# Alternate loading at the start of an attention and MLP block, and where transposed maxima are placed

## The chip, the cores and the metric

The kernel runs on one core of a Trainium2 chip. Its engines work side by side, each through its own instructions in order: TensorE (PE in the profile: matmuls and transposes), VectorE (DVE), ScalarE (ACT), GpSimd (POOL) and SyncE (SP, which here issues all DMAs). The metric is the time of one execution in microseconds on the device; smaller is better. Before the change the median of three runs is 1664.54 us (1664.17 to 1665.02).

## The reference

One transformer block on x of 2048 rows and 512 columns, in float32: layer norm, attention with 32 heads of 16 columns, a residual, layer norm, an MLP with 1792 hidden columns and SiLU, a residual.

```python
def _A_ref(x, wqkv, wo):
    qkv = (x @ wqkv).reshape(B, S, 3, H, Dh)...   # q, k, v per head
    scores = jnp.einsum("bhqd,bhkd->bhqk", q, k) * Dh ** -0.5
    p = _softmax(scores, axis=-1)
    o = jnp.einsum("bhqk,bhkd->bhqd", p, v)
    return o (heads side by side) @ wo

def _B_ref(x, w1, w2):
    return _silu(x @ w1) @ w2

h = x + _A_ref(_layernorm(x), wqkv, wo)
h2 = h + _B_ref(_layernorm(h), w1, w2)
```

## The kernel before, in words

**Precision.** Projections, the output projection and the MLP are made in three products each: an operand is split into a high part (a cast to fp32r, suffix `_h`) and a low part (the operand less its high part, suffix `_l`, made by `low`), and `product` (L123) adds high x high, low x high and high x low over four chunks of 128. Scores are made in float16 from q and k split in the same way and stored three times along the contraction.

**The softmax's maxima.** Before an item (four heads by 512 queries) can be scored, the maximum of each row of its scores is found: `maximum` (L241) makes a 128x512 block of scores into a bank of PSUM (`ps_m`) and DVE reduces it into a column of `mx`. Where all blocks of an item are there, `finish_max` joins the columns and splits the result into two float16 parts (`ns`) on POOL. `place_max` (L287) then transposes `ns` on TensorE into a bank (`ps_n`), copies it to SBUF (`mt`), and SP writes it as two more rows of q (`qs`), so that the matmul of the scores subtracts the maximum itself. In all there are 64 items of 32 to 64 blocks and 33 placements.

**Phases.** First comes block 0 of x (four tiles of 128 rows): statistics, normalization, transposes, and its products with the values' weights. Then `project_qk` and `project_v` run over blocks and column groups. Then come 512 groups of attention, interrupted three times by the output projection and `mlp` for a finished block of rows (`marks`), and a last MLP. The order of work is written out by hand: every instruction of an engine stays in the order of the program (`keep_in_program_order`). Maxima are strewn in between as bursts: `weave` (L381) calls `burst` (L375) after the k-th matmul of a product. `BESIDE_A` puts six maxima behind the sixth of twelve matmuls of a projection; `BESIDE_C` puts three behind the fifth and the twelfth of the first MLP product of a hidden chunk and four behind the eighth of its second product. The banks of kind `sm`, which maxima and `ps_n` take in turn, are six in the later projections and three from attention on.

**When a placement is due.** `one_max` (L340) hands `place_max` to `soon` (L313) outside attention groups, three steps ahead; `tick` (L317), called at the beginning of each projection, each hidden chunk of an MLP and each group, then calls it, ahead of the first matmul of that step. Within attention groups the table `late` does it.

**The start.** `load_x(0, parts=4)` issues four transfers of 256 KB, then come four of the values' weights (`raw_v`), eight of the weights of k and q, and block 1 of x. `idle` makes transposes of the identity that nobody reads. `first_rows(t)` normalizes tile t on DVE and calls `turn_high` (four transposes on TensorE, a copy to `xth` on ACT); `first_products` adds high x high for a tile of rows and some chunks. The high part of the weights, `wv_h`, is made on ACT for chunks 0 and 1 and on POOL for 2 and 3.

Of the kernel before, what the change touches and what calls it, by code (L numbers as in the profile page):

```python
# [20 lines left out]
P = 128  # L21
# [60 lines left out]
def attention_mlp_kernel(ctx: ExitStack, tc: tile.TileContext, x, wqkv, wo, w1, w2, out):  # L82
# [204 lines left out]
    def place_max(piece):  # L287

        i, a = piece
        ns = split.pop(piece)  # L290
        n = ns.shape[1]
        ps = bank("ps_n", "sm", F16)
        tr(ps[:n, :P], ns, ident_h)
        mt = small.tile([32, P], F16, name="mt")[:n]
        if at["attention"]:
            dve("tensor_copy", mt, ps[:n, :P])
        else:
            act("copy", mt, ps[:n, :P])
        for j in range(2):
            dst = qs[i % RING][64 * j + 48:64 * j + 50, slice(None) if a is None else slice(a, a + 1)]  # L300
            dst = dst.rearrange("r a n -> r (a n)").rearrange("r (a b) -> r a b", b=P)
            pin(nc.sync.dma_start(dst, mt[n // 2 * j:n // 2 * (j + 1), :]))
        placed.add(piece)
# [4 lines left out]
            for i in range(ITEMS) for j in range(2)}  # L308
    END = 64 * ITEMS
    at = {"item": 0, "done": 0, "half": 0, "step": 0, "due": 0, "attention": False, "group": None, "ready": 0, "next": 0, "blocks": True}  # L310
    agenda, late = {}, {}

    def soon(steps, fn, *a):  # L313

# [2 lines left out]
    def tick():  # L317
        at["step"] += 1
        for step in [step for step in late if step < at["step"]]:

            finish_rest()
            for i in late.pop(step):
                place_max(i)
        for fn, a in agenda.pop(at["step"], ()):
            fn(*a)

# [13 lines left out]
    def one_max(half=None, ps=None):  # L340

        i = next_item()
        if i == ITEMS:
            return
        if half is None:
            half = at["half"]
            at["half"] = 1 - half
        if at["blocks"]:

            i = min(range(2), key=lambda n: (todo[n, half] or todo[n, 1 - half] or [(n, KC)])[0][1])  # L350
        elif not todo[i, half] and 64 * (i + 2) <= at["ready"] and KC * i - at["next"] > 12:

            i += 1
        half = half if todo[i, half] else 1 - half
        at["done"] += 1
        block = todo[i, half].pop(0)
        piece = piece_of(i, block[3])
        found_all = maximum(*block, ps)

        finish_rest()  # L360
        if found_all:
            steps = due_at(piece)
            g = at["group"]
            if g is None or g + 1 in marks:
                soon(steps, place_max, piece)
                finish_max(piece, g is not None)
                return
            late.setdefault(at["step"] + steps, []).append(piece)
            if steps == WAIT:
                unfinished.append(piece)  # L370
                found_at["step"] = at["step"]
            else:
                finish_max(piece, False)

    def burst(n, *more):  # L375
        for ps in more:
            one_max(ps=ps)
        for _ in range(n - len(more)):
# [29 lines left out]
    with ExitStack() as pa:  # L408
# [88 lines left out]
            turn(xts[b][:, t, :], xth[b][:, :, t * P:(t + 1) * P], xtl[b][:, :, t * P:(t + 1) * P],  # L497
                 "sm" if b == 1 else "st")

        load_x(0, parts=4)  # L500
        for dc in range(DC):
            dma(raw_v[:, dc, :], wqkv[dc * P:(dc + 1) * P, 2 * D:])
        for key in (1, 0):
            for dc in range(DC):
                dma(raw_qk[key][:, dc, :], wqkv[dc * P:(dc + 1) * P, key * D:(key + 1) * D])
# [15 lines left out]
            act("copy", xth[b][:, :, columns(t)], ps)  # L521
            return ps

        idle(24)
        found = [statistics(xts[0][:, t, :]) for t in range(2)]
        turned, ps_vs = [], []

        def first_rows(t):
            normalize(xts[0][:, t, :], xts[0][:, t, :], *found[t])
            turned.append(turn_high(0, t))  # L530

        def first_products(t, *chunks):
            if t == len(ps_vs):
                ps_vs.append(bank("ps_v", "st" if t < 3 else "sm"))
            for c in chunks:
                mm(ps_vs[t], xth[0][:, c, columns(t)], wv_h[:, c, :], start=c == 0, stop=False)

        first_rows(0)
        idle(8)
        for c in range(2):  # L540
            act("copy", wv_h[:, c, :], raw_v[:, c, :])
        found += [statistics(xts[0][:, t, :]) for t in range(2, 4)]
        for c in range(2, 4):
            pool("tensor_copy", wv_h[:, c, :], raw_v[:, c, :])
        first_rows(1)
        first_products(0, 0)
        first_rows(2)
        first_products(0, 1)
        first_rows(3)
        for chunks in ((0, 1), (2,), (3,)):  # L550
            for t in range(2):
                if t or chunks != (0, 1):
                    first_products(t, *chunks)
        for t in range(2, 4):
            first_products(t, *range(DC))
        for c in range(DC):
            low(wv_l[:, c, :], raw_v[:, c, :], wv_h[:, c, :])
        for t in range(4):
            low(xtl[0][:, :, columns(t)], turned[t], xth[0][:, :, columns(t)])

        keys = [n for n in range(NG) if n % 2]
# [8 lines left out]
                normalize(xts[1][:, t - 1, :], xts[1][:, t - 1, :], *found.pop(t - 1))  # L570
        for t in range(4):
            for c in range(DC):
                mm(ps_vs[t], xth[0][:, c, columns(t)], wv_l[:, c, :], start=False, stop=False)
                mm(ps_vs[t], xtl[0][:, c, columns(t)], wv_h[:, c, :], start=False, stop=c == DC - 1)
            act("copy", va[:, t, :, 0:DH], ps_vs[t].rearrange("p (h d) -> p h d", d=DH))
            if t == 0:
                load_x(2)
# [625 lines left out]
```

## Time and profile before

| | |
|---|---|
| median of three runs | 1664.54 us |
| profiled execution | 1664.61 us, span 1662.8 us |
| TensorE busy, matmuls | 1649.5 us, 99% of the span |
| DVE busy | 1453.2 us, 87% |
| ACT busy | 1235.6 us, 74% |
| POOL busy | 396.7 us, 24% |
| placements: copies `mt` on DVE / ACT | 30 / 3 |

A row of the timeline gives start, duration, engine, line, operation, what it writes and reads, and a count; in brackets stands how long the engine had been idle before it and what ended that. Nearly all matmuls go through one helper line, so they are told apart by the names of their tiles. Matmuls overlap: the duration of one (0.39 us for a 128x512 one in fp32r) is longer than its distance to the next (0.23 us), and the distances between starts are what counts. In the chain (the work that ended last, followed back), a piece such as "PE pv L89 x7" is seven matmuls in sequence.

### The profile page before, as it was taken

What the parts mean: (1) busy time and instruction counts of PE and PEld (TensorE: products, weight loads), DVE (VectorE), ACT (ScalarE), POOL (GpSimd) and SP (SyncE); (2) the same over time, 40 slices, a digit from 0 to 9 for tenths busy, and PEclk for the clock granted to TensorE, in tenths of its full rate; (3) what the DMA queues carried; (4) which work ended last, traced back from release to release, by engine and by line L of the source; (5) the groups of instructions that cost most, each with busy time, mean ns of one, the idle gap of its engine ahead of it and who ended that gap; (6) DMA issues with size and microseconds to landing.
All of it is one profiled execution on the core that took longest, in us unless ns stands there. A gap on an engine that the chain in (4) does not pass through costs nothing.

```text
span 1662.8 us, 28572 instructions
## 1 busy us (share of the span) xinstructions
PE 1649.5 (99%) x10551; PEld 649.5 (39%) x10551; DVE 1453.2 (87%) x2403; ACT 1235.6 (74%) x2435; POOL 396.7 (24%) x584
## 2 busy tenths in 40 slices
PE   9999999999999999999999999999999999999999
PEld 7666422222245532222245532222245642222387
DVE  7899999999988889999988889999978769999443
ACT  5323799999953389999952379999962389999743
POOL 5423311211234301211244311211235311111100
PEclk9999999999999999999999999999999999999999
DMA  5444411211232211121222111121232211100222
GB/s 199 109 100 140 120 32 37 57 33 36 69 76 67 58 50 34 41 51 33 60 76 79 58 50 32 37 58 32 61 68 77 69 50 34 33 12 21 65 77 82
DMA packets 104408, 102.85 MB, mean 62 GB/s; under 512 B 22736, under 2 KB 81168, under 8 KB 104268
## 3 DMA queue, kind: packets, MB, share of 16 engines
q1 hardware_dynamic: 104268, 101.02, 22.4%
q8 instruction: 83, 1.36, 0.4%
q14 instruction: 57, 0.47, 0.1%
HBM read 77.72 MB, written 17.29 MB: 57 GB/s over the span
## 4 chain that ended last, share of the span: by engine, by line
PE 91%; DVE 4%; ACT 3%; issue 1%; DMA 1%; POOL 1%; SPq 0%; DVEq 0%; POOLq 0%
PE pv L89 35%; PE ps_s L89 21%; PE ps_m L89 11%; PE ps_acc L89 10%; PE ps_qk L89 5%; PE ps_wo L89 3%; PE ps_w L89 3%; ACT pt L103 3%; PE ps_v L89 3%; DVE mx L253 2%; PE ps_tr L92 1%; SPq L109 0%; DVE pvs L106 0%; POOL ri L96 0%; PE ps_n L92 0%
## 5 line engine op out<-in xcount | busy, mean ns | idle before, releaser
L253 DVE TENSOR_REDUCE mx<-ps_m 128x1 f32<-128x512 f32 x2011 | 1261.2, 684 | 79.5 <-PE ps_m L89 50.2
L103 ACT ACTIVATE pt<-ps_s 128x512 f32<-128x512 f32 x2048 | 1010.9, 609 | 32.0 <-PE ps_m L89 18.6
L89 PE MATMUL pv<-pt,va 128*17 128x512 f32 x4096 | 537.6, 598 | 1.4 <-DVE pv L106 0.5
L89 PE MATMUL ps_s<-qs,ks 64*128 64x512 f16 x2048 | 532.1, 379 | 2.8 <-ACT pt L103 1.6
L89 PE MATMUL ps_m<-ks,qs 48*128 48x512 f16 x2011 | 504.8, 380 | 0.9 <-DVE mx L253 0.7
L89 PEld LDWEIGHTS <-ks 64*128 64x128 f16 x2048 | 150.2, 95 | 547.2 <-issue 434.2
L96 POOL TENSOR_TENSOR ri<-rc,minus 128x16 f32<-128x16 f32 x31 | 90.8, 2929 | 306.1 <-DMA rc<-dn 306.1
L89 PEld LDWEIGHTS pv<-pt,va 128*17 128x17 f32 x4096 | 69.0, 95 | 215.3 <-issue 201.6
L89 PEld LDWEIGHTS <-qs 48*128 48x128 f16 x2048 | 119.0, 94 | 63.4 <-issue 57.3
L103 ACT CAST w2h<-w 128x512 fp32r<-128x512 f32 x56 | 34.7, 619 | 99.5 <-PE ps_acc L89 99.5
L103 ACT ACTIVATE g<-pv 128x512 f32<-128x512 f32 x39 | 23.3, 597 | 100.5 <-PE pv L89 100.5
L89 PE MATMUL ps_acc<-w2l,gh 128*128 128x512 f32 x224 | 92.8, 414 | 0.0
L89 PE MATMUL ps_acc<-w2h,gh 128*128 128x512 f32 x224 | 91.9, 410 | 0.0
L96 POOL TENSOR_TENSOR w2l<-w,w2h 128x512 fp32r<-128x512 f32 x42 | 53.9, 1283 | 148.2 <-ACT w2h L103 148.2
L89 PE MATMUL ps_acc<-w2h,gl 128*128 128x512 f32 x224 | 88.2, 394 | 0.0
L106 DVE TENSOR_TENSOR gl<-g,gh 128x512 fp32r<-128x512 f32 x53 | 37.2, 701 | 56.2 <-ACT gh L103 56.2
L103 ACT ACTIVATE ks<-ps_qk,qk_s 128x512 f32<-128x512 f32 x30 | 20.7, 689 | 68.8 <-PE ps_qk L89 66.9
L96 POOL TENSOR_SCALAR nm<-nm 128x16 f32<-128x16 f32 (+1 forms) x50 | 12.7, 254 | 232.2 <-DVE nm L264 229.2
L89 PE MATMUL pv<-htl,w1h 128*128 128x512 f32 x156 | 65.5, 420 | 0.0
L89 PE MATMUL pv<-hth,w1h 128*128 128x512 f32 x156 | 62.4, 400 | 0.0
L89 PE MATMUL pv<-hth,w1l 128*128 128x512 f32 x156 | 61.4, 393 | 0.0
L96 POOL TENSOR_TENSOR w1l<-w,w1h 128x512 fp32r<-128x512 f32 x42 | 54.2, 1291 | 11.1 <-ACT w1h L103 11.1
(138 smaller groups left out, 1395.3 us busy)
## 6 DMA issues: line engine op xcount, KB each, us to landing
w<-in_B_w_dram SPq DMA_DIRECT2D x112, 256.0 KB
ks<-kd SPq DMA_DIRECT2D x120, 192.0 KB
qs<-qd SPq DMA_DIRECT2D x128, 48.0 KB
kd<-sh SPq DMA_DIRECT2D x16, 256.0 KB
qd<-sh SPq DMA_DIRECT2D x16, 256.0 KB
hx<-in_A_x_dram SPq DMA_DIRECT2D x16, 256.0 KB
ot<-pvs SPq DMA_DIRECT2D x124, 32.0 KB
den<-dr SPq DMA_DIRECT2D x124, 32.0 KB
```

What stands on the lines that cost most here:

```text
L89: tc.keep_in_program_order(nc.tensor.matmul(*a, **k))
L92: tc.keep_in_program_order(nc.tensor.transpose(*a))
L96: tc.keep_in_program_order(getattr(nc.gpsimd, op)(*a, **k))
L103: pin(getattr(nc.scalar, fn)(*a, **k))
L106: pin(getattr(nc.vector, fn)(*a, **k))
L253: pin(nc.vector.tensor_reduce(mx[piece][:, j, a % n, qt, kb:kb + 1], ps, axis=AX.X, op=ALU.max))
```

## The change

Two things are changed.

At the start, x tiles and the values' weights are loaded alternately, tile 0, weights 0, tile 1, weights 1 and so on; statistics, the casts of the weights (now all four on ACT), normalization, transposes and first products are written in another order, in which the products with a tile follow its transposes closely. The low parts of the weights are made on DVE and POOL by turns, and the low products of a tile take the low part of x first and the low part of the weights after it.

Outside attention groups, a placement that is due is kept in a list (`in_bursts`). `burst` looks there first, so that `place_max` comes right ahead of the burst's maxima, between the matmuls of a product; where no burst comes in the step in which it is due, the next `tick` places it. With the condition in `place_max`, the copy to `mt` is on ACT whenever no attention group is running, in the MLPs too. Of the 33 placements, three are in projections (two of them move from the front of a projection to its burst, one to the front of the projection after), six in MLPs (two in the first hidden chunk, four in others; all move to a burst), and two more slip from the first attention group behind an MLP to the next. Six copies `mt` go from DVE to ACT.

```diff
@@ -292,7 +292,7 @@
         ps = bank("ps_n", "sm", F16)
         tr(ps[:n, :P], ns, ident_h)
         mt = small.tile([32, P], F16, name="mt")[:n]
-        if at["attention"]:
+        if at["group"] is not None:
             dve("tensor_copy", mt, ps[:n, :P])
         else:
             act("copy", mt, ps[:n, :P])
@@ -308,7 +308,7 @@
             for i in range(ITEMS) for j in range(2)}
     END = 64 * ITEMS
     at = {"item": 0, "done": 0, "half": 0, "step": 0, "due": 0, "attention": False, "group": None, "ready": 0, "next": 0, "blocks": True}
-    agenda, late = {}, {}
+    agenda, late, in_bursts = {}, {}, []
 
     def soon(steps, fn, *a):
 
@@ -321,6 +321,7 @@
             finish_rest()
             for i in late.pop(step):
                 place_max(i)
+        place_due(1)
         for fn, a in agenda.pop(at["step"], ()):
             fn(*a)
 
@@ -362,7 +363,7 @@
             steps = due_at(piece)
             g = at["group"]
             if g is None or g + 1 in marks:
-                soon(steps, place_max, piece)
+                in_bursts.append((at["step"] + steps, piece))
                 finish_max(piece, g is not None)
                 return
             late.setdefault(at["step"] + steps, []).append(piece)
@@ -372,7 +373,13 @@
             else:
                 finish_max(piece, False)
 
+    def place_due(slack=0):
+        while in_bursts and in_bursts[0][0] + slack <= at["step"]:
+            place_max(in_bursts.pop(0)[1])
+
     def burst(n, *more):
+
+        place_due()
         for ps in more:
             one_max(ps=ps)
         for _ in range(n - len(more)):
@@ -497,9 +504,9 @@
             turn(xts[b][:, t, :], xth[b][:, :, t * P:(t + 1) * P], xtl[b][:, :, t * P:(t + 1) * P],
                  "sm" if b == 1 else "st")
 
-        load_x(0, parts=4)
-        for dc in range(DC):
-            dma(raw_v[:, dc, :], wqkv[dc * P:(dc + 1) * P, 2 * D:])
+        for t in range(4):
+            dma(xts[0][:, t, :], x[t * P:(t + 1) * P, :])
+            dma(raw_v[:, t, :], wqkv[t * P:(t + 1) * P, 2 * D:])
         for key in (1, 0):
             for dc in range(DC):
                 dma(raw_qk[key][:, dc, :], wqkv[dc * P:(dc + 1) * P, key * D:(key + 1) * D])
@@ -521,13 +528,17 @@
             act("copy", xth[b][:, :, columns(t)], ps)
             return ps
 
-        idle(24)
-        found = [statistics(xts[0][:, t, :]) for t in range(2)]
-        turned, ps_vs = [], []
+        found, turned, ps_vs = [], [], []
+
+        def first_statistics(t):
+            found.append(statistics(xts[0][:, t, :]))
 
         def first_rows(t):
             normalize(xts[0][:, t, :], xts[0][:, t, :], *found[t])
             turned.append(turn_high(0, t))
+
+        def first_weights_of(c):
+            act("copy", wv_h[:, c, :], raw_v[:, c, :])
 
         def first_products(t, *chunks):
             if t == len(ps_vs):
@@ -535,27 +546,34 @@
             for c in chunks:
                 mm(ps_vs[t], xth[0][:, c, columns(t)], wv_h[:, c, :], start=c == 0, stop=False)
 
+
+        idle(24)
+        first_statistics(0)
+        first_weights_of(0)
+        first_statistics(1)
+        first_weights_of(1)
         first_rows(0)
         idle(8)
-        for c in range(2):
-            act("copy", wv_h[:, c, :], raw_v[:, c, :])
-        found += [statistics(xts[0][:, t, :]) for t in range(2, 4)]
-        for c in range(2, 4):
-            pool("tensor_copy", wv_h[:, c, :], raw_v[:, c, :])
+        first_statistics(2)
+        first_weights_of(2)
+        first_products(0, 0, 1)
         first_rows(1)
-        first_products(0, 0)
+        first_weights_of(3)
+        first_products(0, 2)
+        first_products(1, 0, 1, 2)
+        first_statistics(3)
         first_rows(2)
-        first_products(0, 1)
+        first_products(0, 3)
+        first_products(1, 3)
+        first_products(2, *range(DC))
         first_rows(3)
-        for chunks in ((0, 1), (2,), (3,)):
-            for t in range(2):
-                if t or chunks != (0, 1):
-                    first_products(t, *chunks)
+        first_products(3, *range(DC))
+
+        for c in range(DC):
+            low(wv_l[:, c, :], raw_v[:, c, :], wv_h[:, c, :], "pool" if c % 2 else "dve")
+            if c % 2 == 0:
+                low(xtl[0][:, :, columns(c // 2)], turned[c // 2], xth[0][:, :, columns(c // 2)])
         for t in range(2, 4):
-            first_products(t, *range(DC))
-        for c in range(DC):
-            low(wv_l[:, c, :], raw_v[:, c, :], wv_h[:, c, :])
-        for t in range(4):
             low(xtl[0][:, :, columns(t)], turned[t], xth[0][:, :, columns(t)])
 
         keys = [n for n in range(NG) if n % 2]
@@ -570,8 +588,9 @@
                 normalize(xts[1][:, t - 1, :], xts[1][:, t - 1, :], *found.pop(t - 1))
         for t in range(4):
             for c in range(DC):
-                mm(ps_vs[t], xth[0][:, c, columns(t)], wv_l[:, c, :], start=False, stop=False)
-                mm(ps_vs[t], xtl[0][:, c, columns(t)], wv_h[:, c, :], start=False, stop=c == DC - 1)
+                mm(ps_vs[t], xtl[0][:, c, columns(t)], wv_h[:, c, :], start=False, stop=False)
+            for c in range(DC):
+                mm(ps_vs[t], xth[0][:, c, columns(t)], wv_l[:, c, :], start=False, stop=c == DC - 1)
             act("copy", va[:, t, :, 0:DH], ps_vs[t].rearrange("p (h d) -> p h d", d=DH))
             if t == 0:
                 load_x(2)
```

## The prediction

> **What bounds the kernel now.** I read the totals and the chain first, then the stretches that the change touches: the opening microseconds, one projection and two MLP iterations around a transposed set of maxima.
>
> ```profile
> PE 1649.5 (99%) x10551; PEld 649.5 (39%) x10551; DVE 1453.2 (87%) x2403; ACT 1235.6 (74%) x2435; POOL 396.7 (24%) x584
> ...
> PEclk9999999999999999999999999999999999999999
> ...
> PE 91%; DVE 4%; ACT 3%; issue 1%; DMA 1%; POOL 1%; SPq 0%; DVEq 0%; POOLq 0%
> ```
>
> TensorE sets the end: 91% of the chain, and its clock is full in every slice. So a change pays only where it takes a matmul, a switch of operand type, or a stall out of TensorE's order. The opening, as the timeline shows it:
>
> ```profile
> 3.57 0.69 DVE L106 BATCH_NORM_STATS2 st<-ks 128x6 f32<-128x512 f32 x1 [1.54 <-DMA ks<-in_A_x_dram]
> ...
> 6.09 0.66 PE L92 MATMUL ps_tr<-ident,ks 128*128 128x128 f32 x4
> ...
> 6.78 0.59 ACT L103 CAST xth<-ps_tr 128x512 fp32r<-128x512 f32 x1 [4.78 <-PE ps_tr L92]
> ...
> 8.13 0.66 PE L92 MATMUL ps_tr<-ident,ks 128*128 128x128 f32 x4 [0.52 <-DVE ks L106]
> ...
> 8.55 0.48 PE L89 MATMUL ps_v<-wv_h,xth 128*128 128x512 f32 x1
> ...
> 10.12 3.45 PE L89 MATMUL ps_v<-wv_h,xth 128*128 128x512 f32 x14
> ...
> 12.07 0.62 ACT L103 CAST wqk_h<-va 128x512 fp32r<-128x512 f32 x1 [1.07 <-DMA va<-in_A_wqkv_dram]
> 12.40 2.47 DVE L106 TENSOR_TENSOR xtl<-ps_tr,xth 128x512 fp32r<-128x512 f32 x4
> ...
> 13.41 0.39 PE L89 MATMUL ps_v<-wv_l,xth 128*128 128x512 f32 x1
> ...
> 20.75 1.04 PE L92 MATMUL ps_tr<-ident,ks 128*128 128x128 f32 x8
> ```
>
> The reader is to see that TensorE's real work starts at 8.13 and then never stops. From there to 20.75 it does 12 transposes and 48 products. The last 32 products take 20.75 - 13.41 = 7.34, or 0.23 each; a set of four transposes takes about 0.46 of its order (8.55 less 8.13 is 0.42, more with the switch back). 48 x 0.23 + 3 x 0.46 = 12.4 of the 12.6 us. There is nothing to save behind 8.13, only the start itself. The stretch behind it, and what the loads bring per 1.5 us slice of the first 60 us:
>
> ```profile
> 13.40:21.00 7.60, 7.60 (x36) 6.21 (x35) 7.26 (x16) 7.10 (x19) 3.03 (x7) 1.00 0.75 272
> ```
>
> ```profile
> GB/s 0 186 381 352 363 384 395 402 388 392 391 382 187 4 0 5 0 129 133 0 262 30 100 105 117 105 184 155 288 288 385 226 46 76 95 96 98 96 319 103
> ```
>
> In the window row the numbers after the length are busy times of PE, PEld, DVE, ACT and POOL: TensorE 7.60 of 7.60.
>
> **The change, part 1: the start.** Nothing is added or removed but the engine of two casts (`wv_h` 2 and 3 from POOL to ACT) and of two subtractions (`wv_l` 1 and 3 from DVE to POOL). The four tiles of x and the first four rows of weights are loaded alternately, so x tiles come as transfers 1, 3, 5, 7 instead of 1 to 4. Summing the GB/s row, 256 KB have moved at about 2.9 us, and the tile was usable at 3.57, so 0.6 behind; twelve have moved at about 10.6 and the last was used at 12.07, 1.4 behind. With lags of 0.6 to 1.4, tile x1 comes at 4.9 to 5.7, weights 1 at 5.6 to 6.4, x2 at 6.4 to 7.2, weights 2 at 7.1 to 7.9, x3 at 7.8 to 8.6, weights 3 at 8.6 to 9.4. I take the early ends first, as the first tile shows them. DVE now does both sets of statistics ahead of the first normalization: 4.95 + 0.69 + 0.18 + 0.55 puts its end at 6.35, the transposes at 6.4, and `xth` 0 at 7.65 (6.09 to 7.37 is 1.28 from transpose to usable). So products 0,0 and 0,1 start at about 7.7, 0.4 ahead of the 8.13 of now. But each later set of transposes stands right in front of the products that need it, and TensorE takes its matmuls in order. Of the 1.28 us from transposes to `xth`, the four transposes fill 0.46; behind set 1 stands one product (0.23), behind set 2 two (0.46), behind set 3 none. The stalls are 0.6, 0.36 and 0.82, 1.8 together, and they are new: now the sets at 8.13, 8.86 and 9.71 run ahead of the products. Net 1.8 - 0.4 = 1.4 later at the first product with a low part. By then everything else is there: on DVE the lows need 0.62 each (2.47 for four) and start near 9.8; the last one waits for `xth` 3 at 13.7 and ends at 14.4, while its products come after 16 others. The reordered low products (all `xtl` first, then all `wv_l`) are the same 32. ACT is the second watch: it starts `wqk_h` after `xth` 3, at 13.7 instead of 12.07, and has 7.10 of 7.60 us busy behind that. It falls 1.6 behind and TensorE 1.4, so the values' eviction may be 0.2 late, which the eight transposes cover. Late landings add up to 0.8, and full cover of the stalls would give a gain of 0.4: bounds -0.4 to +2.5. I take **+1.4**. It passes on whole: all that follows is released by TensorE until DVE's bursts of maxima at 49 us, and these are released by TensorE too.
>
> **Part 2: transposed maxima in projections.** These rows stand around one of them (`ps_n`):
>
> ```profile
> 115.53 0.82 PE L89 MATMUL ps_m<-ks,qs 48*128 48x512 f16 x6
> ...
> 117.89 0.23 PE L92 MATMUL ps_n<-ident_h,ns 128*32 128x128 f16 x1
> ...
> 118.76 0.62 ACT L103 CAST sh<-ks 128x512 f16<-128x512 f32 x1
> ...
> 119.28 0.25 ACT L103 COPY mt<-ps_n 32x128 f16<-32x128 f16 x1
> ...
> 119.64 0.82 PE L89 MATMUL ps_m<-ks,qs 48*128 48x512 f16 x6
> 120.06 6.19 DVE L253 TENSOR_REDUCE mx<-ps_m 128x1 f32<-128x512 f32 x10 [0.42 <-PE ps_m L89]
> ...
> 123.34 0.83 PE L89 MATMUL ps_m<-ks,qs 48*128 48x512 f16 x6
> ```
>
> From burst to burst it is 119.64 - 115.53 = 4.11 with a `ps_n` and 123.34 - 119.64 = 3.70 without: the lone f16 transpose between fp32r products costs 0.41, and DVE then idles 0.42. Moved directly ahead of the burst, the switch is paid once, and `ps_n` adds only its own slot, 0.15 (553.12 to 553.27, below). Six banks are rotated, so only the sixth maximum needs the one of `ps_n`, 0.84 later; `mt` is done 0.26 + 0.25 after `ps_n`, as ACT's cast is over by then. Gain 0.41 - 0.15 = 0.26. Of three projections two move to a burst; the third only goes to the next boundary between projections, at no gain. **-0.5**. The queue of SP gets the two small row writes one projection later, behind two writes of q; the item that reads them starts after the projections, so I cost that at nothing.
>
> **Part 3: MLPs.** Iterations from the chain, then rows of one with a `ps_n`:
>
> ```profile
> 539.26 1.82 PE pv L89 x7
> ...
> 547.02 1.82 PE pv L89 x7
> ...
> 555.24 1.83 PE pv L89 x7
> ...
> 563.02 1.82 PE pv L89 x7
> ```
>
> ```profile
> 546.42 0.60 PE L89 MATMUL ps_m<-ks,qs 48*128 48x512 f16 x3
> ...
> 546.95 0.51 PE L89 MATMUL pv<-htl,w1h 128*128 128x512 f32 x1
> ...
> 553.12 0.22 PE L92 MATMUL ps_n<-ident_h,ns 128*32 128x128 f16 x1
> 553.27 0.51 PE L89 MATMUL pv<-hth,w1h 128*128 128x512 f32 x1
> 553.47 0.62 ACT L103 CAST w1h<-w 128x512 fp32r<-128x512 f32 x1
> ...
> 554.18 0.20 DVE L106 COPY mt<-ps_n 32x128 f16<-32x128 f16 x1
> ```
>
> Iterations take 7.76 and 7.78, the one with `ps_n` 8.22: 0.45 more. Moved to the burst after five products, `ps_n` would begin five products later, at 553.12 + 5 x 0.23 or just ahead of it, about 554.2. There are three banks here: `ps_n` and two maxima fill them, and the third maximum needs `ps_n`'s bank. Its `mt` is now on ACT: 0.26 + 0.25 + 0.05 = 0.56 after `ps_n`, where without `ps_n` the third maximum started at 0.28. So the burst is 0.28 longer, and the gain is 0.45 - 0.28 = 0.17. ACT's cast of `w1h` ends at 554.09, just ahead. Four such places: **-0.7**. Two places stand ahead of the first product of an MLP:
>
> ```profile
> 484.60 0.68 DVE L106 TENSOR_TENSOR htl<-ps_tr,hth 128x512 fp32r<-128x512 f32 x1
> ...
> 485.88 0.22 PE L92 MATMUL ps_n<-ident_h,ns 128*32 128x128 f16 x1
> ...
> 486.16 0.21 DVE L106 COPY mt<-ps_n 32x128 f16<-32x128 f16 x1 [0.89 <-PE ps_n L92]
> ...
> 487.82 0.69 DVE L253 TENSOR_REDUCE mx<-pv 128x1 f32<-128x512 f32 x1 [1.45 <-PE ps_m L89]
> ```
>
> DVE idles 0.89 and 1.45 there, so its bursts begin as much earlier as TensorE reaches them. The front loses `ps_n` and a switch (0.41), the burst of four gains 0.15; 0.25 is left each, **-0.5**. The six `mt` copies that leave DVE for ACT are worth nothing: DVE has these gaps. Two more places only slip by one attention group, between the same neighbours: nothing. The floor for all places is that eight prices vanish, 0.41 x 8 = -3.3; the ceiling is in the first rival.
>
> **Sum.** +1.4 - 0.5 - 0.7 - 0.5 = -0.3. The profiled execution took 1664.61 (span 1662.8), 0.07 above the median of 1664.54: 1664.3.
>
> **Rivals.** *Slower: the third maximum waits behind casts.* If `ps_n` reaches the six MLP bursts while ACT is in a cast, `mt` waits up to 0.62 more, and TensorE with it, as the third maximum and all products behind it are in order: 0.28 + 0.62 - 0.43 = +0.47 each, +2.8. With +1.4 and -0.5 that is +3.7, 1668.3. It needs nearly the whole cast at every place; 554.09 against 554.2 speaks against it. *Faster: places become free and the start is covered*: -3.3 - 0.4 = -3.7, 1660.9. The idle of DVE speaks for it, the three banks against. *The change of the start does nothing*, because loads, not the order, set it: 1664.6 - 1.7 = 1662.9; 8.13 waited for DVE, not for a load, which speaks against. *The clock falls in the new stalls*: with products twice as long for 16 of them, 16 x 0.23 = +3.7 on top, 1668.0; against it, TensorE already stood still 0.52 before 8.13 at full clock. The Trainium skill, "TensorE: Matmul & The Clock Gate", Part 1, has the clock halved after an idle window of about 3.4 us, and under "A second HAM failure mode" also by short idling between groups. By its second rule the start would cost some 1.7 us more, by my estimate from that window; by the first nothing. The trace agrees with the first: 0.52 idle, clock full.
>
> **How the numbers follow.** 0.2% is 3.3 us, about what a measurement of this kernel can tell from no change. My forecast with the start anywhere in its bounds, the untouched start among it, stays within that: 0.81. Free places 0.09. Casts in front 0.07, the clock 0.03. The range 1662.0 to 1666.6 takes in the start's bounds (-1.8 to +1.1 about my +1.4) with half of the places' gain missing or doubled; what it leaves out at both ends is some 0.2.
>
> **What would show it.** In the changed profile the first real product begins near 7.7, with waits on `xth` near 9, 11 and 13, and the eight transposes now at 20.75 begin near 22.1. Projection bursts with a `ps_n` stand 3.85 apart, MLP iterations with one take 8.05. The prediction is wrong if the transposes at the start find other work behind them, if x1 comes much later than 5.7, or if `mt` in the MLP starts later than 0.3 after `ps_n`.

## The result and the profile after

The changed kernel takes 1667.67 us (median of 18 runs, 1666.97 to 1668.39); the kernel before took 1664.74 us in the same sessions (18 runs, 1664.17 to 1665.22). The ratio is 1.0017, with a 95% interval of 1.0011 to 1.0024: 2.9 us slower, above the range that was predicted. The profiled executions stand 2.8 apart, 1667.41 against 1664.61, so the traces can be set beside each other.

Three lines of the page of the changed kernel, its totals, the clock and the shares of the chain:

```profile
PE 1651.3 (99%) x10551; PEld 650.8 (39%) x10551; DVE 1452.7 (87%) x2395; ACT 1238.1 (74%) x2443; POOL 398.3 (24%) x584
...
PEclk9999999999999999999999999999999999999999
...
PE 93%; DVE 3%; ACT 3%; issue 1%; POOL 0%; DVEq 0%; POOLq 0%
```

TensorE still sets the end, executes as many matmuls, and has its full clock in every slice. So the 2.8 us are stalls and switches in its order, and they can be found by following how far the changed kernel lags at the same instruction. The rows from which the table is read stand below it or in the prediction; the others are the same pieces of the chains of the two kernels.

| place (start before) | lag there, us | what it adds |
|---|---|---|
| eight transposes of block 1 (20.75) | 1.91 | +1.91 the start |
| burst ahead of the first placement in a projection (115.60), burst behind it (119.70) | 1.93, 1.72 | -0.21 |
| four projections on, burst ahead of the second (134.53) | 1.84 | +0.12 |
| burst behind the second (138.63), late projections (176.66) | 1.63, 1.67 | -0.21, +0.04 |
| first matmuls of attention (188.88) | 2.75 | +1.08 the third placement |
| first chunk of MLP 1 (483.36 to 492.62) | 2.75, 2.94 | +0.19 |
| later chunk of MLP 1 (547.02 to 555.24) | 2.95, 2.84 | -0.11 |
| first chunk of MLP 2 (861.22 to 870.49), then a later one (924.88 to 933.11) | 2.85, 3.03; 3.04, 2.93 | +0.18, -0.11 |
| attention behind MLP 2 (971.28 to 981.59) | 2.94, 2.78 | -0.16 |
| MLP 3 (1247.08), two later chunks up to 1318.37 | 2.77, 2.59 | -0.09, -0.10 |
| last output projection (1563.08 to 1575.02) | 2.59, 2.86 | +0.27 |
| last piece (1650.57) | 2.82 | |

The named steps add up to 1.91 - 0.26 + 1.08 + 0.37 - 0.41 - 0.16 + 0.27 = 2.80. The step of -0.16 comes where a placement slips by one group: in the kernel before, the first of the two rows below, it stands between float32 products of the MLP and scores; now it stands behind products with the values and takes 0.04 instead of 0.16.

```profile
974.53 0.16 PE ps_n L92
```

```profile
980.06 0.04 PE ps_n L92
```

All six traces with the changed placements there have this step, and none of the others. The +0.27 ahead of the last MLP stands in only two of these six traces, this one and that of the third placement's experiment below; the others have 0.05 or less there, so I don't count it as the work of the change, and its cause is open.

The opening, as the timeline of the changed kernel shows it:

```profile
1.53 5.38 PE L92 MATMUL ps_i<-ident 128*128 128x128 f32 x24 [1.53 <-POOL ident masks.py:199]
...
4.99 0.69 DVE L106 BATCH_NORM_STATS2 st<-ks 128x6 f32<-128x512 f32 x1 [0.56 <-DMA ks<-in_A_x_dram]
...
5.82 0.51 DVE L106 TENSOR_SCALAR ks<-ks,mv,rs 128x512 f32<-128x512 f32 x1
...
6.70 0.64 PE L92 MATMUL ps_tr<-ident,ks 128*128 128x128 f32 x4
...
8.02 0.72 PE L89 MATMUL ps_v<-wv_h,xth 128*128 128x512 f32 x2
...
8.58 0.65 PE L92 MATMUL ps_tr<-ident,ks 128*128 128x128 f32 x4
...
8.99 0.47 PE L89 MATMUL ps_v<-wv_h,xth 128*128 128x512 f32 x1
...
9.91 0.96 PE L89 MATMUL ps_v<-wv_h,xth 128*128 128x512 f32 x3 [0.45 <-ACT xth L103]
...
11.07 0.72 PE L89 MATMUL ps_v<-wv_h,xth 128*128 128x512 f32 x2
...
11.99 1.20 PE L89 MATMUL ps_v<-wv_h,xth 128*128 128x512 f32 x4 [0.20 <-ACT xth L103]
...
13.02 0.60 PE L92 MATMUL ps_tr<-ident,ks 128*128 128x128 f32 x4
...
14.29 1.19 PE L89 MATMUL ps_v<-wv_h,xth 128*128 128x512 f32 x4 [0.67 <-ACT xth L103]
15.33 1.08 PE L89 MATMUL ps_v<-wv_h,xtl 128*128 128x512 f32 x4
...
22.66 1.04 PE L92 MATMUL ps_tr<-ident,ks 128*128 128x128 f32 x8
```

Behind each set of transposes TensorE waits for `xth`. Measured by starts (a matmul's order slot is 0.23 us), the stalls are 9.91 - 8.99 - 0.23 = 0.69, 11.99 - 11.07 - 0.46 = 0.46, and 14.29 - 13.02 - 0.46 = 0.81: 1.96 together. The 32 low products behind them take 22.66 - 15.33 = 7.33 as before (7.34).

A placement in a projection, from the chain of the changed kernel:

```profile
117.53 0.75 PE ps_m L89 x6
118.28 2.99 PE ps_qk L89 x12
121.27 0.16 PE ps_n L92
121.42 0.75 PE ps_m L89 x6
122.18 2.97 PE ps_qk L89 x12
125.14 0.75 PE ps_m L89 x6
```

`ps_n` takes 0.15 of TensorE's order right ahead of the burst, and the burst is no longer for it. From burst to burst it is 121.42 - 117.53 = 3.89, where the same pieces of the kernel before give 119.70 - 115.60 = 4.10. But part of this gain is lost again: from 119.70 to 134.53, four projections without a placement took 14.83, and now they take 14.95 (121.42 to 136.37). Their products stand a few ns farther apart, and I have no cause for it. Of twice 0.21, 0.26 is left by 176.66. The last projection ahead of attention, where the third placement now stands, from the timeline of the changed kernel:

```profile
181.74 0.37 PE L89 MATMUL ps_m<-ks,qs 48*128 48x512 f16 x1 [0.23 <-DVE mx L253]
...
185.28 0.23 PE L92 MATMUL ps_n<-ident_h,ns 128*32 128x128 f16 x1
...
185.50 0.70 ACT L103 ACTIVATE ks<-ps_qk,qk_s 128x512 f32<-128x512 f32 x1
...
186.28 0.62 ACT L103 CAST sh<-ks 128x512 f16<-128x512 f32 x1
186.80 0.25 ACT L103 COPY mt<-ps_n 32x128 f16<-32x128 f16 x1
187.10 0.37 PE L89 MATMUL ps_m<-ks,qs 48*128 48x512 f16 x1 [0.41 <-ACT mt L103]
...
191.63 1.05 PE L89 MATMUL pv<-pt,va 128*17 128x512 f32 x8 [0.47 <-DVE pv L106]
```

`mt` is made 1.5 us after its `ps_n`, because ACT first does an eviction and a cast that stand ahead of it in its queue. A maximum of the same projection needs the bank of `ps_n`, and TensorE stands 0.41 for it, with the products behind it. In the kernel before, that `ps_n` stood ahead of an earlier projection and held nothing up: the lag is 1.67 on either side of that place (178.33 against 176.66, 182.04 against 180.37). The first row tells why: with `ps_n` gone from there, TensorE waits 0.23 for DVE to free a bank. The burst of three maxima there takes 1.41 to the next product (180.63 to 182.04), where it took 1.05 before (179.32 to 180.37): what left TensorE's order came back as a wait.

Last, the MLPs. For a first chunk I take the distance from the last 24 matmuls of attention's values ahead of the MLP (x24) to the second part of the first product of the chunk behind it (x7). These are the two pieces in the chain of the kernel before for MLP 1, with a placement at the front of its first chunk, and below them for MLP 3, whose first chunk has none:

```profile
483.36 2.70 PE pv L89 x24
...
492.62 1.80 PE pv L89 x7
```

```profile
1237.87 2.70 PE pv L89 x24
...
1247.08 1.82 PE pv L89 x7
```

The same two pieces of MLP 1 in the chain of the changed kernel, and below them two later iterations, the first with a placement in its burst, the second without:

```profile
486.11 2.70 PE pv L89 x24
...
495.56 1.82 PE pv L89 x7
```

```profile
549.97 1.82 PE pv L89 x7
...
558.08 1.82 PE pv L89 x7
...
565.86 1.82 PE pv L89 x7
```

Before, the first chunk took 492.62 - 483.36 = 9.26 with a placement at its front and 9.21 without any: at the front the placement cost 0.05. Now it takes 9.45. A later chunk takes 8.11 with a placement in its burst, where it took 8.22, and 7.78 without one.

### The profile page after: what moved, and what is told of

Same layout as the page of the kernel before. It is cut to its first block, busy times and chain, and to the rows that moved or that the text cites. A ratio compares the mean times of both kernels' runs of the same rounds, so it can differ in the third digit from the quotient of the medians.

```text
span 1665.6 us, 28572 instructions
## 1 busy us (share of the span) xinstructions
PE 1651.3 (99%) x10551; PEld 650.8 (39%) x10551; DVE 1452.7 (87%) x2395; ACT 1238.1 (74%) x2443; POOL 398.3 (24%) x584
## 3 DMA queue, kind: packets, MB, share of 16 engines
q8 instruction: 83, 1.36, 0.3%
## 4 chain that ended last, share of the span: by engine, by line
PE 93%; DVE 3%; ACT 3%; issue 1%; POOL 0%; DVEq 0%; POOLq 0%
PE pv L89 36%; PE ps_s L89 21%; PE ps_m L89 11%; PE ps_acc L89 10%; PE ps_qk L89 5%; PE ps_w L89 3%; PE ps_wo L89 3%; ACT pt L103 3%; PE ps_v L89 3%; DVE mx L253 2%; PE ps_tr L92 1%; DVE pvs L106 0%; PE ps_i L92 0%; PE ps_n L92 0%; DVE ot L106 0%
```

## The experiments

Medians of an experiment are set against the kernel before in the same session (1664.65, 1664.67, 1664.81 or 1664.95 us). Beside the time I use stages, which the traces show much more exactly: *start*, at which block 1's eight transposes begin (20.75 before, 22.66 after); *projections*, from there to the first matmuls of attention (168.13 before, 168.97 after); *first chunk* (9.26, 9.45) and *later chunk* (8.22, 8.11) of MLP 1, as above. The start is the exception: each trace is one execution, and the landing of the loads moves it (last section), so for the start the medians decide.

### The two parts apart

The start of the changed kernel in the kernel before, with all placements as before (the part of the diff from the loads to the low products):

```diff
-        load_x(0, parts=4)
...
+        first_statistics(0)
+        first_weights_of(0)
...
+                mm(ps_vs[t], xth[0][:, c, columns(t)], wv_l[:, c, :], start=False, stop=c == DC - 1)
```

> The kernel before with the changed start alone (loads, order, engines of the casts and low parts); placements as before. Theory: the start costs 1.9 us by the eight transposes of block 1 (20.75 to 22.66) and nothing behind it takes that back, so 1666.6 us against 1664.7, ratio 1.0011, and the third placement stands where it stood, with attention beginning 1.9 later than before (first product with the values near 190.8). Rival: the 1.1 us that the changed kernel loses between the projections and attention comes from the later start (maxima and scores falling differently), not from the placement; then this kernel is near 1667.7 and attention begins near 191.7.

Measured: 1666.59 us, +1.94 (ratio 1.0012, 1.0003 to 1.0021). Start 22.92, projections 168.14, first chunk 9.26, later chunk 8.21. So the start alone loses two thirds, all of it ahead of block 1's transposes; a later start changes nothing in the projections, which it would if the 1.08 ahead of attention were its echo.

The placements of the changed kernel with the start of the kernel before (the other part of the diff):

```diff
-        if at["attention"]:
+        if at["group"] is not None:
...
+        place_due(1)
...
-                soon(steps, place_max, piece)
+                in_bursts.append((at["step"] + steps, piece))
...
     def burst(n, *more):
+        place_due()
```

> The changed placements alone; the start as before. Theory (sum of stages read from the two traces): two projections -0.33, the third placement +1.08, two first hidden chunks +0.32, four other chunks -0.41: +0.7, so 1665.4 us, with attention beginning near 189.6 instead of 188.88. Rival: placements are worth what was forecast (-1.7, 1663.0) and the whole loss belongs to the start.

Measured: 1665.23 us, +0.58 (1.0004, 0.9995 to 1.0013); the interval holds 1, so the stages have to show it. Projections 168.94, first chunk 9.46, later chunk 8.10, the changed kernel's stages. (Block 1's transposes begin at 21.65 in this trace, though the start is that of before: statistics waited there for a late tile of x.) The steps of the table give -0.26 + 1.08 + 0.37 - 0.41 - 0.16 = +0.62. The two medians add up to +2.5 of the 2.9; the other tenths have no place.

### The third placement

In the changed kernel, this placement alone goes back to the front of the projection before:

```diff
-        place_due(1)
+        place_due(0 if in_bursts and in_bursts[0][1] == (2, None) else 1)
```

> The changed kernel, with the third placement put back in front of the last projection but one (all else as changed). Theory: its new place, ahead of the last projection's scores and maxima, costs 1.08 and its old one nothing, because DVE was the limit there: 1666.6 us, attention beginning near 190.6. Rival: the place is not the cause, the same time as the changed kernel, 1667.7; second rival, that every placement in front of a projection costs 0.41: then 1667.0.

Measured: 1666.43 us (ratio to the kernel before 1.0010, 1.0001 to 1.0019), 1.2 below the changed kernel. Projections 167.89, which is 1.08 less than in the changed kernel and 0.24 less than before, with first and later chunks as in the changed kernel. So the 1.08 is this one placement, and what is left in the projections is the gain of the other two.

The same placement where the changed kernel has it, with its copy on DVE:

```diff
-        if at["group"] is not None:
+        if at["group"] is not None or piece == (2, None):
             dve("tensor_copy", mt, ps[:n, :P])
```

> The changed kernel, with the copy of the third placement on DVE instead of ACT, at its new place. Theory: 0.8 of its 1.08 us is the last maximum of the last projection waiting for its bank while the copy stands behind an eviction and a cast on ACT (0.70 and 0.62); DVE had nothing to do there for 0.35, so the copy comes at once and 0.8 comes back: 1666.9 us, and no wait of 0.41 ahead of that maximum. Rival: the wait is for the bank as such (six banks for eight tiles), and stays: 1667.7.

Measured: 1666.52 us (1.0013, 1.0003 to 1.0023). Projections 168.23: 0.74 of the 1.08 are gone. Its timeline:

```profile
184.92 0.23 PE L92 MATMUL ps_n<-ident_h,ns 128*32 128x128 f16 x1
...
185.53 0.20 DVE L106 COPY mt<-ps_n 32x128 f16<-32x128 f16 x1
...
185.96 0.38 PE L89 MATMUL ps_m<-ks,qs 48*128 48x512 f16 x2
```

The copy is done 0.81 after `ps_n` begins, not 1.77, and TensorE no longer waits for it. So about 0.74 of the step was ACT's queue. The other 0.34 stays with the place; I take it for the price of a `ps_n` where TensorE's order is the limit, which no run shows apart.

### Loads, order, and what covers the transposes

Only the loads alternate; all the rest is as before:

```diff
-        load_x(0, parts=4)
-        for dc in range(DC):
-            dma(raw_v[:, dc, :], wqkv[dc * P:(dc + 1) * P, 2 * D:])
+        for t in range(4):
+            dma(xts[0][:, t, :], x[t * P:(t + 1) * P, :])
+            dma(raw_v[:, t, :], wqkv[t * P:(t + 1) * P, 2 * D:])
```

> The kernel before with the alternate loads alone; engines' orders as before. Theory: the loads alone are dear with the old order, since it wants statistics of tiles 2 and 3 ahead of the second normalization and these tiles land at 7.2 and 8.5: the second set of transposes goes from 8.13 to about 9.9, and block 1's transposes from 20.75 to 22.5, 1666.4 us. Rival (loads are free, order is the cost): 20.75 and 1664.7.

Measured: 1666.57 us, +1.9 (1.0011, 1.0002 to 1.0021); start 22.88. In its timeline the statistics now wait for x, and the transposes for them:

```profile
8.72 0.69 DVE L106 BATCH_NORM_STATS2 st<-ks 128x6 f32<-128x512 f32 x1 [0.39 <-DMA ks<-in_A_x_dram]
...
10.12 0.66 PE L92 MATMUL ps_tr<-ident,ks 128*128 128x128 f32 x4 [1.44 <-DVE ks L106]
```

The second set of transposes begins at 10.12 where the kernel before had it at 8.13. With the order of before, alternate loads are paid in full.

The opposite: the order of the changed kernel, with x loaded first as before. To the first experiment:

```diff
-        for t in range(4):
-            dma(xts[0][:, t, :], x[t * P:(t + 1) * P, :])
-            dma(raw_v[:, t, :], wqkv[t * P:(t + 1) * P, 2 * D:])
+        load_x(0, parts=4)
+        for dc in range(DC):
+            dma(raw_v[:, dc, :], wqkv[dc * P:(dc + 1) * P, 2 * D:])
```

> The kernel before with the changed order and engines of the start, but x loaded first as before. Theory: the stalls behind each set of transposes stay, and the casts of the weights stand ahead of the first copy of x on ACT and wait for the weights (6.4, 7.1): block 1's transposes at about 22.5, 1666.5 us. Rival (the later x tiles are the cost, order is free): 20.9 and 1664.9.

Measured: 1667.30 us, +2.6 (1.0017, 1.0007 to 1.0027); start 22.88.

```profile
6.52 1.24 ACT L103 CAST wv_h<-va 128x512 fp32r<-128x512 f32 x2 [4.52 <-DMA va<-in_A_wqkv_dram]
...
8.30 0.73 PE L89 MATMUL ps_v<-wv_h,xth 128*128 128x512 f32 x2 [0.65 <-ACT xth L103]
...
14.53 1.19 PE L89 MATMUL ps_v<-wv_h,xth 128*128 128x512 f32 x4 [0.68 <-ACT xth L103]
```

Here all of x is early and the stalls behind the transposes remain: the last products wait 0.68 for `xth` as in the changed kernel (0.67). The stalls belong to the order. Together loads and order cost 1.9, so their prices (1.9 and 2.6 by the medians) don't add: either alone holds the start up by at least as much. The trace is of the fastest of this kernel's ten executions, 1666.59 us, so its start is earlier than most.

If the order is the cause, covering the transposes must take the stalls away. From the first experiment, each of the last two sets of transposes goes ahead of a lot of products of another tile, and all low parts are made on DVE:

```diff
         first_products(0, 2)
-        first_products(1, 0, 1, 2)
         first_statistics(3)
         first_rows(2)
+        first_products(1, 0, 1, 2)
         first_products(0, 3)
         first_products(1, 3)
-        first_products(2, *range(DC))
         first_rows(3)
+        first_products(2, *range(DC))
         first_products(3, *range(DC))
+        low(xtl[0][:, :, columns(0)], turned[0], xth[0][:, :, columns(0)])
         for c in range(DC):
-            low(wv_l[:, c, :], raw_v[:, c, :], wv_h[:, c, :], "pool" if c % 2 else "dve")
-            if c % 2 == 0:
-                low(xtl[0][:, :, columns(c // 2)], turned[c // 2], xth[0][:, :, columns(c // 2)])
-        for t in range(2, 4):
+            low(wv_l[:, c, :], raw_v[:, c, :], wv_h[:, c, :])
+        for t in range(1, 4):
```

> The changed start with its loads, but the third and fourth set of transposes moved one lot of products ahead, and all low parts on DVE as before; placements as before. Theory: stalls behind transposes are the cost; with products of another tile behind each set they are covered but for the first, low products begin near 13.9 instead of 15.33 and block 1's transposes near 21.2: 1665.2 us. Rival: tiles come too late for any order: 22.6 and 1666.6.

Measured: 1665.17 us, +0.50 (1.0003, 0.9994 to 1.0013), 1.4 less than with the order of the changed kernel; start 21.49.

```profile
8.51 0.73 PE L89 MATMUL ps_v<-wv_h,xth 128*128 128x512 f32 x2
...
11.85 0.60 PE L92 MATMUL ps_tr<-ident,ks 128*128 128x128 f32 x4
12.21 2.12 PE L89 MATMUL ps_v<-wv_h,xth 128*128 128x512 f32 x8
...
14.16 1.08 PE L89 MATMUL ps_v<-wv_h,xtl 128*128 128x512 f32 x4
```

Eight products stand behind the last transposes, and they run through: 14.16 - 12.21 = 1.95 for eight, where 8 x 0.23 = 1.84. From the first product to block 1's transposes it takes 21.49 - 8.51 = 12.98, in the changed kernel 22.66 - 8.02 = 14.64. That is 1.66 less, of 1.96 of stalls, at alternate loads, but with two changes: the order and the low parts, which the next run takes apart.

The same with two of the weights' low parts on POOL again, as the changed kernel has them (the lower half of that diff is left out):

```diff
         for c in range(DC):
-            low(wv_l[:, c, :], raw_v[:, c, :], wv_h[:, c, :])
+            low(wv_l[:, c, :], raw_v[:, c, :], wv_h[:, c, :], "pool" if c % 2 else "dve")
```

> The start with the transposes moved ahead (loads alternate, placements as before), but two of the weights' low parts on POOL as in the changed kernel. Theory: POOL's two subtractions (2.72 us) hold DVE's operations beside them (1.50 and 1.77 us instead of 0.55 and 0.68), the fourth normalization comes 0.9 late, and with the transposes ahead TensorE feels it: 0.6 later than with all low parts on DVE, measured from the third set of transposes on (block 1's transposes 11.9 instead of 11.3 behind it). Rival: DVE's long operations have nothing to do with POOL, and both kernels agree to 0.1.

Measured: 1665.83 us, +1.0 (1.0007, 0.9998 to 1.0016); start 21.86. From the third transposes to block 1's it takes 12.00, against 11.29 with all low parts on DVE.

```profile
10.50 2.70 POOL L96 TENSOR_TENSOR wv_l<-va,wv_h 128x512 fp32r<-128x512 f32 x2
10.57 1.50 DVE L106 TENSOR_SCALAR ks<-ks,mv,rs 128x512 f32<-128x512 f32 x1 [0.77 <-POOL rs L96]
```

A normalization takes 1.50 beside POOL's subtractions, and the fourth transposes wait for it (they begin at 12.12, it ends at 12.07); without them it takes 0.55. So the move to POOL, which the prediction left out of its sum, costs about half a microsecond in an order in which nothing else is late, and covering the transposes alone brings 0.9 of the 1.9 by the medians. In the changed kernel the move hides behind the stalls: the same normalization ends at 12.10 (10.60 + 1.50), and the fourth transposes begin at 13.02, when the products ahead of them are through.

### The first chunk and the copies in the MLPs

In the changed kernel the two placements of first chunks go back to the front, with their copies on DVE:

```diff
-        if at["group"] is not None:
+        if at["group"] is not None or at.get("front"):
...
         for f in range(FC):
-            tick()
+            at["front"] = f == 0
+            tick(1 if f else 0)
+            at["front"] = False
```

> The changed kernel with the two placements of the first hidden chunks put back in front of the chunk (copy on DVE). Theory: in front they cost nothing, since the switch from the products with the values to fp32r is paid there anyway, and at the burst they cost 0.16 each: 0.3 less than the changed kernel, about 1667.4 us; from the last products with the values before an MLP (x24) to the first pv x7 of that MLP 9.25 us as before, not 9.45. Rival: the 0.16 comes from something else in that stage (the weights' loads), and stays.

Measured: first chunk 9.25, as before the change, later chunk 8.11. That shows the step. The time shows nothing: 1667.65 us (1.0019, 1.0010 to 1.0028) is no gain. In the profiled execution x landed later (start 23.43 where the changed kernel, with the same code there, has 22.66), which is more than the 0.4 in question; whether that holds for the others isn't known.

Copies of all MLP placements on DVE, in the changed kernel:

```diff
-        if at["group"] is not None:
+        if at["attention"]:
             dve("tensor_copy", mt, ps[:n, :P])
```

> The changed kernel with all six MLP copies on DVE, as before the change, the places unchanged. Theory: the engine of the copy is of no account there (ACT is free when the copy comes; DVE too, give or take 0.1): 1667.7 us, MLP iterations with a placement 8.10 as in the changed kernel. Rival: ACT's copy is the gain, and iterations take 8.2 again, or DVE's copy waits behind maxima and they take over 8.3.

Measured: 1667.19 us, 0.5 less than the changed kernel (ratio to before 1.0016, 1.0006 to 1.0025; the two intervals overlap). First chunk 9.39 and later chunk 8.06, 0.05 less each: so in the stages the engine matters a little even where ACT is free, and the two account for 2 x 0.06 + 4 x 0.05 = 0.3.

### What is left of the change

The start of before; placements go into bursts only in two projections and four later chunks of MLPs, with the copy on ACT, and stay at the front elsewhere (lines set against the changed kernel; those of the start are left out):

```diff
-        if at["group"] is not None:
+        if at["attention"] and not in_burst:
...
-    def tick():
+    def tick(slack=0):
...
-        place_due(1)
+        place_due(slack)
...
-                tick()
+                tick(1 if 8 * g + m - 12 < 18 else 0)
...
         for f in range(FC):
-            tick()
+            tick(1 if f else 0)
```

> The start as before; placements at bursts only in the two projections and in the four MLP chunks behind the first (there with the copy on ACT); the third placement, those of the first hidden chunk and those in attention as before. Theory: only the gains are left, -0.33 and -0.41, so 1664.0 us, ratio 0.9996. Rival: the small gains of the stages are taken back later (by waits in attention), 1664.7.

Measured: 1663.92 us, -0.7 (0.9997, 0.9988 to 1.0006); projections 167.89, later chunk 8.11. The stages give (167.89 - 168.13) - 4 x 0.11 = -0.68.

The same with the MLP copies on DVE:

```diff
-        if at["attention"] and not in_burst:
+        if at["attention"]:
```

> The selective kernel (two projections and the four later MLP chunks at bursts, all else as before) with the four MLP copies on DVE, whose copy is 0.04 us shorter than ACT's. Theory: MLP iterations with a placement take 8.06 instead of 8.11 and 8.22, so 0.2 less than the selective kernel, 0.9 less than before: 1663.8 us against 1664.7. Rival: no difference from the selective kernel, 0.7 less than before.

Measured: 1663.95 us against 1664.95 in its session, -1.0 (0.9994, 0.9985 to 1.0003); projections 167.93, later chunk 8.06. The stages give -0.20 - 4 x 0.16 = -0.84. This is the largest gain of the study over the kernel before in the same session; the selective kernel with the copy on ACT has about the same median (1663.92), and the two can't be told apart by time. Against the changed kernel it is some 3.9 us, taken over the kernel before (-1.0 against +2.9); that it beats the kernel before is what the median and the stages say, while the interval of its time still holds 1.

## Why the prediction was wrong, step by step

**What bounds the kernel** was right: TensorE's order, at full clock. All of the loss is found there.

**The start (+1.4) was right in its mechanism and too small.** Three stalls were named with 0.6, 0.36 and 0.82, and they measure 0.69, 0.46 and 0.81: 1.96 for 1.8. The first product was put at 7.7 and came at 8.02. The second tile of x was used at 4.99, where I had taken the early end, 4.95, so the landing was no part of it; and the normalization ended at 5.82 + 0.51 = 6.33 (6.35 forecast; its terms add up to 6.37). The missing 0.3 lies right behind it: the transposes began at 6.70, not 6.4, because the 24 transposes of the identity stood ahead of them. In this execution these took 5.38 from 1.53 on, and the last began at 6.49; in the trace before it was 4.48 and 5.73. No row tells why. With a first product 0.1 ahead of 8.13 instead of 0.4, 1.96 of stalls give the 1.9 that is measured. The experiments show the stalls to be the cause: covered, 1.4 of the 1.9 come back with all low parts on DVE, and 0.9 with POOL's, where a wait of 0.6 for the held-up normalization takes their place.

**The projections (-0.5): the bursts brought half, and the third placement failed.** The two bursts gained 0.21 each at their place for 0.26, but 0.16 was lost again in the projections behind them, which the sum didn't have: -0.26 is left of -0.52. The failing step is that the third placement "only goes to the next boundary between projections, at no gain". I looked at what it leaves and not at where it lands. What it left was worth nothing, because DVE was the limit there; where it lands it costs 1.08, 0.74 of it by the copy behind an eviction and a cast of ACT. I had this mechanism as the slower rival, but priced it for the MLPs, where `mt` starts 0.27 after `ps_n`, as forecast. It happened once, in a projection. This one step is the largest of the miss, 1.08 of some 3.1 by the traces (-0.3 forecast, +2.8 measured); first chunks have 0.9, the start 0.5, later chunks 0.3 and the bursts 0.3. Without it the time would be 1666.6, the upper end of the range, and the run with this placement at the front took 1666.43.

**Later chunks of the MLPs (-0.7): right in kind, -0.4.** Iterations take 8.11 for a forecast of 8.05. With the copy on DVE they take 8.06: the rest is the time of ACT's copy.

**First chunks (-0.5): wrong sign, +0.4.** I took the price of a lone `ps_n` between fp32r products, 0.41, for a place that is no such place: ahead of it stand the 24 matmuls of attention's values, and the products begin 2.73 behind the first of these with a `ps_n` between (483.29 to 486.02) and 2.70 without (1237.80 to 1240.50). MLP 3 stood in the trace of before and would have told it: 9.21 against 9.26, so 0.05 could be saved. In the burst it costs 9.45 - 9.21 = 0.24.

**The slipped placements (nothing): -0.16.** "Between the same neighbours" was not so behind MLP 2, as the two rows under the table show.

**The other rivals.** Free places did not come: each costs 0.2 to 0.3 in an MLP's burst and 0.15 in a projection's. That the start changes nothing is refuted. The clock did not fall in the stalls, this stretch of the changed kernel having 1.00 in the column ahead of the last two, with 0.65 of 5.40 us without TensorE's work:

```profile
8.00:13.40 5.40, 4.75 (x26) 3.30 (x24) 4.60 (x7) 2.18 (x4) 4.67 (x6) 1.00 1.05 396
```

The Trainium skill, "TensorE: Matmul & The Clock Gate", "A second HAM failure mode", has frequent short idling between groups of matmuls make the clock swing. The trace does not show it for three stalls of up to 0.81 us in six microseconds: 1.00 throughout. The column alone would not settle it, since it has 1.00 also between 1.5 and 6.5 us, where the identity's transposes stand some 0.21 apart, while those from 7.18 on stand 0.11 apart. The distances do: behind the stalls the products stand 0.23 apart, 32 in 7.33 us, as before.

**The range.** The start's bounds and half of the places' gain (0.85), laid about the forecast of 1664.3, give 1661.6 to 1666.3; the stated 1662.0 to 1666.6 is the same width laid about 1664.6, the time before.

## What to carry to other kernels

Price an operation that is moved twice, by what it cost where it stood and by what it costs where it lands; both can be read in the trace before, best from a neighbour of the same kind without the operation (here the MLP that has no placement). Here a small copy that frees a bank cost what its engine's queue had ahead of it (0.74), and the matmul that needed the bank passed that on to everything behind it. And a transpose whose result comes back through another engine needed work of another tile behind it in TensorE's order; without that, an earlier start of 0.1 was paid with 1.96 of stalls.

## What was not expected of the hardware

DVE takes longer beside POOL's subtractions. In the changed kernel too, beside POOL's two subtractions of 1.36 us each, DVE's normalization takes 1.50 us instead of 0.55 and its subtraction 1.77 instead of 0.68:

```profile
10.53 2.72 POOL L96 TENSOR_TENSOR wv_l<-va,wv_h 128x512 fp32r<-128x512 f32 x2
10.60 1.50 DVE L106 TENSOR_SCALAR ks<-ks,mv,rs 128x512 f32<-128x512 f32 x1 [0.76 <-POOL rs L96]
...
12.02 1.77 DVE L106 TENSOR_TENSOR wv_l<-va,wv_h 128x512 fp32r<-128x512 f32 x1
```

DVE's two end 0.2 and 0.5 us after POOL's two (11.89 and 13.25, by halves of 2.72). The Trainium skill, "SBUF — State Buffer", "SBUF: two separate sides", has the two engines share a pair of ports under an exclusive lock that the first to start keeps for its whole instruction: a DVE instruction in a mode that takes two ports, or with two SBUF inputs against a POOL instruction that reads SBUF, waits until POOL's has ended. The trace agrees in part: DVE's end follows POOL's in both cases, but by less than DVE's instructions take alone (0.2 against 0.55, 0.5 against 0.68).

The landing of the same loads moves by over a microsecond between executions. With the loads and code of the changed kernel at the start, the second tile of x was used at 4.81, 4.99, 5.15, 5.53, 5.60 and 6.11 us in six traces, and block 1's transposes began at 22.27, 22.66, 22.92, 23.23, 22.92 and 23.43. With those of the kernel before, four traces have them at 20.75, 20.89, 21.65 and 21.77. Single traces of the start therefore differ by more than most terms of this study; stages that begin behind it agree between kernels to about 0.1 us.
